# Sparse attention and two feed-forward layers on one core: a second buffer for the exponentials of a local unit, a free ScalarE order in the third tile, and high priority for the operations between h and y

## The chip, the cores and the metric

The program runs on one core of one Trainium2 chip. The metric is the device time of one execution in microseconds (us); lower is better. Several runs of a kernel agree within about 0.2%.

## The reference, cut to what matters

Four batches of 576 tokens pass through an attention with eight heads of 64 columns. Heads 0 to 3 see the last 32 positions, heads 4 to 7 every 32nd position. Two feed-forward layers follow.

```python
scores = scale * np.matmul(q, k.transpose(0, 1, 3, 2))
rel = pos[:, None] - pos[None, :]
mask_local = (rel >= 0) & (rel < 32)
mask_strided = (rel >= 0) & (pos[None, :] % 32 == pos[:, None] % 32)
attn = softmax(np.where(masks, scores, -1e9))      # local for heads 0..3, strided for 4..7
x = (attn @ v) as 2304 tokens x 512
h = np.maximum(x @ w_in, 0.0);  x = h * h @ w_out                    # 512 -> 2048 -> 512
h = x @ w_in2;  g = np.maximum(h, 0) + alpha * np.minimum(h, 0);  out = g @ w_out2
```

All inputs are 32-bit floats.

## The kernel before

**Tiles and steps.** The first layer works on seven tiles of tokens: the first three, t = 0, 1, 2, have 256 tokens, the next four 384. The second layer has six tiles of 384. The hidden width of 2048 is cut into 16 pieces f of 128. A step is one pair of tile and piece. Steps 0 to 31 alternate between tiles 0 and 1, steps 32 to 47 are the third tile (t = 2), steps 48 to 111 the tiles 3 to 6, and steps 112 to 207 the second layer.

**What one step does.** Every operand is split into a high part and a rest, and each product is three matmuls. `emit_h` makes h of a step with 12 matmuls (L566) in the one PSUM bank "h". `emit_g` makes g and its high part gh: in the first layer three ScalarE instructions, Relu (L578), Square into gh (L579), Square into g (L580). `emit_gl` makes the rest gl with one VectorE subtraction (L594). `emit_y` adds 8 matmuls with gh and 4 with gl into the banks y (L620). In the second layer `emit_g` has two Relus and a copy on ScalarE (L583, L584, L588) and one VectorE operation (L585). The tags g, gh and gl have two buffers each. The next h needs the bank that the Relu reads, so a Relu that comes late holds up the next h.

**Attention beside the steps.** The attention of a later tile is spread over the steps of an earlier one. A local unit goes through scores (PE, L245), `softmax_a` (VectorE: scaling and mask into e, L259, and the maximum, L263), `softmax_b` (ScalarE: one Exp for each block with its sum, L267), `softmax_c` (VectorE: L274, L275; then the division, from tile 3 on three ScalarE copies with a scale, L282, before that one VectorE product, L277), `turn` (PE transposes, L289, which read e), `turn_copy` (ScalarE, L293), `values` (PE, L299), `emit_hi` (ScalarE, L308) and `emit_lo` (VectorE, L315). The tag e has one buffer: the next unit's L259 waits until the transposes of the unit before have read e. The strided heads are done on VectorE alone in many products and sums (L450, L457, L491, L498), which fill its time. Units for tile 3 run in steps 32 to 47, with first stages in steps 32, 34, 37 and 40.

**Weights.** The first layer's weights arrive as 64-bit words and are converted in four parts, on ScalarE (L159, L162, L185) and VectorE (L171, L172, L175, L191), just ahead of their first use.

**What sets the order.** `run` emits the parts of step n in this order: loads, gl of n, `front`, h of n + 1, `fill`, the matmuls of attention, g of n + 1, `tail`, y of n. A scheduler then orders each engine's instructions before the program runs: among those that are ready in its own account of time it takes the one that was emitted first. `manual_schedule` names engines that keep the order of emission instead. Before the change that is SyncE alone in steps 0 to 31, and SyncE and ScalarE from step 32 on. Within `tc.high_priority()` instructions count as if they had been emitted at the start of the program. TensorE and VectorE are left to the scheduler throughout. Once set, the order of an engine is kept on the chip.

Of the kernel before, what the change touches and what calls it, by code (L numbers as in the profile page):

```python
# [16 lines left out]
P = 128  # L17
# [53 lines left out]
def attn_moe_moe2(  # L71
# [39 lines left out]
    NF = w_in1.shape[0]  # L111
# [31 lines left out]
    def load_w(layer, f):  # L143

        t = wpool.tile([P, 2, 512, 2], U32, tag=f"w{f}", name="wraw")
        for h in range(2):
            src = W[layer][h][f].bitcast(U32).rearrange("p (f t) -> p f t", t=2)
            nc.sync.dma_start(out=t[:, h], in_=src)
        raws[layer, f] = t
# [58 lines left out]
    class Unit:  # L208


        bufs = None
# [40 lines left out]

        def softmax_a(self):
            n = self.n
            self.e = self.new("e", [P, 3, 96], bufs=1)[:, 0:n]
            self.st = apool.tile([P, 3, 4], F32, tag="st", name="stat", bufs=4)[:, :, 0:n]
            s = self.s[:, 0:96 * n].rearrange("p (n c) -> p n c", c=96)
            m = mfirst if self.first else mloc
            nc.vector.scalar_tensor_tensor(  # L259
                out=self.e, in0=s, scalar=SCALE,  # L260
                in1=m.unsqueeze(1).to_broadcast([P, n, 96]), op0=ALU.mult, op1=ALU.add,
            )
            nc.vector.tensor_reduce(out=self.st[:, 0, :], in_=self.e, op=ALU.max, axis=AX.X, negate=True)  # L263
# [284 lines left out]
    steps = [(0, t, f) for t, f in FIRST]  # L548
# [6 lines left out]
    def cols_of(n):  # L555
        return COLS[steps[n][1]] if n < SECOND else T

    def emit_h(n):
        l, t, f = steps[n]
        xh, xl = x_tile(t) if l == 0 else x2[t]  # L560
        w = wslot[l, f]
        h = psum("h")
        for c in range(NC):
            whi, wlo = w[:, 0, c * P:(c + 1) * P], w[:, 1, c * P:(c + 1) * P]
            for i, (a, b) in enumerate(((whi, xh), (whi, xl), (wlo, xh))):
                nc.tensor.matmul(  # L566
                    h[:, 0:b.shape[2]], a, b[:, c, :], start=(c == 0 and i == 0), stop=(c == NC - 1 and i == 2)
                )
        hs[n] = h

    def emit_g(n):
        l, t, f = steps[n]
        m = cols_of(n)
        h = hs.pop(n)[:, 0:m]
        g = gpool.tile([P, T], F32, tag="g", name="g")[:, 0:m]
        gh = gpool.tile([P, T], F32R, tag="gh", name="gh")[:, 0:m]
        if l == 0:
            nc.scalar.activation(out=g, in_=h, func=AF.Relu)  # L578
            nc.scalar.activation(out=gh, in_=g, func=AF.Square)  # L579
            nc.scalar.activation(out=g, in_=g, func=AF.Square)  # L580
        else:
            u = spool.tile([P, T], F32, tag="pr", name="u", bufs=2)
            nc.scalar.activation(out=g, in_=h, func=AF.Relu)  # L583
            nc.scalar.activation(out=u, in_=h, func=AF.Relu, scale=-1.0)  # L584
            nc.vector.scalar_tensor_tensor(  # L585
                out=g, in0=u, scalar=nalpha[:, f:f + 1], in1=g, op0=ALU.mult, op1=ALU.add
            )
            nc.scalar.activation(out=gh, in_=g, func=AF.Copy)  # L588
        g_sb[n] = (g, gh)

    def emit_gl(n):
        g, gh = g_sb[n]
        gl = gpool.tile([P, T], F32R, tag="gl", name="gl")[:, 0:cols_of(n)]
        nc.vector.tensor_tensor(  # L594
            out=gl, in0=g, in1=gh.bitcast(F32), op=ALU.subtract
        )
        g_sb[n] = (gh, gl)
# [70 lines left out]
    def at(when, n, fn, *args):  # L668
        when.setdefault(n, []).append((fn, args))

    def emit(when, n):
        for fn, args in when.get(n, []):
            fn(*args)
# [79 lines left out]
    def run(ns):  # L753
        for n in ns:
            l, t, f = steps[n]
            emit(starts, n)
            emit(loads, n)
            emit_gl(n)
            emit(front, n)
            if n + 1 < len(steps):  # L760
                emit_h(n + 1)
            emit(fill, n)
            emit(tensor_part, n)
            if n + 1 < len(steps):
                emit_g(n + 1)
            emit(tail_part, n)
            emit_y(n)
            if f == NF - 1:
                evac(t, l)

    outs = {}
    with tc.manual_schedule(engines={mybir.EngineType.SP}):
        def part(tag, *sizes):

            whole = wpool.tile([P, sum(sizes)], F32, tag=tag, name=f"att_{tag}")
            return [whole[:, sum(sizes[:i]):sum(sizes[:i + 1])] for i in range(len(sizes))]

        masks, de11 = part("w11", 224, 512)
        mfirst, mstr = masks[:, 0:96], masks[:, 96:224]
        bufs = {}  # L780
        for t, tags in enumerate((("w7", "w8", "w9", "w10"), ("w15", "w14", "w13", "w12"))):
            n = D * (t + 1)
            a = part(tags[0], 640, 640, 384, 384)
            v = part(tags[1], *(512,) * 4)
            pt = part(tags[2], *(512,) * 4)
            d = part(tags[3], *((512, 512, 256, 256) if t == 0 else (768, 768, 512)))
            for p in range(2):
                bufs[t, "L", p] = {
                    "qk": a[p].rearrange("p (n c) -> p n c", c=D + 96), "v": v[p][0:96].rearrange("p (n c) -> p n c", c=P),
                    "e": a[2 + p].rearrange("p (n c) -> p n c", c=96), "pt": pt[p][0:96],  # L790
                }
                bufs[t, "D", p] = {
                    "qk": d[p], "v": v[2 + p][0:n].rearrange("p (n c) -> p n c", c=P),
                    "e": d[2 + p] if t == 0 or p == 0 else de11, "pt": pt[2 + p][0:n],
                }
        units = []
        for t, kind in ORDER:
            p = sum(isinstance(x, Unit if kind == "L" else Dense) and x.t == t for x in units)
            if kind == "L":
                units.append(Unit(t, p, 0))  # L800
                units[-1].bufs = bufs[t, "L", p]
            else:
                units.append(Dense(t, p, bufs[t, "D", p]))

        def load_consts():
            nc.sync.dma_start(out=ident, in_=consts[:, 0:128])
            nc.sync.dma_start(out=mloc, in_=consts[:, 128:224])
            nc.sync.dma_start(out=masks, in_=consts[:, 224:448])

        for i, x in enumerate(units):  # L810
            x.load_qk()
            if i == 0:
                load_consts()
            if i > 0:
                units[i - 1].load_v()
            for f, w in enumerate(LOAD_AFTER):
                if w == i:
                    load_w(0, f)
        units[-1].load_v()
        for f, w in enumerate(LOAD_AFTER):  # L820
            if w >= len(units):
                load_w(0, f)
        plan()

        todo = []
        for i, unit in enumerate(units):
            for j, (name, tick) in enumerate(STAGES):
                banks = BANKS.get(name)
                args = (banks[i % len(banks)],) if banks else ()
                todo.append((i + tick + (BACK if unit.t else 0), 1, i, j, getattr(unit, name), args))  # L830
        for f, ticks in enumerate(EARLY):
            for j, (fn, tick) in enumerate(zip((convert_a, convert_b, convert_c, convert_d), ticks)):
                todo.append((tick, 0, f, j, fn, (0, f)))
        for tick, *_, fn, args in sorted(todo, key=lambda x: x[:4]):
            n = sum(tick >= x for x in TICKS)
            if n:
                at(starts, n - 1, fn, *args)
            else:
                fn(*args)
        emit_h(0)  # L840
        emit_g(0)
        run(range(2 * NF))
    with tc.manual_schedule(engines={mybir.EngineType.SP, mybir.EngineType.Activation}):
        run(range(2 * NF, len(steps)))


_OUTS = [((2304, 512), "float32")]
# [104 lines left out]
```

## Time and profile before

| | |
|---|---|
| median of 3 runs | 895.06 us (894.0 to 895.51) |
| the profiled execution, its own time | 895.83 us |
| its span in the profile | 894.0 us, so 1.83 us lie around it |
| TensorE matmul busy | 870.4 us (97% of the span) |
| VectorE busy | 553.5 us (62%) |
| ScalarE busy | 455.1 us (51%) |
| mean granted TensorE clock | 0.996 |

The span runs from the first to the last instruction. PE is TensorE's matmul, PEld its weight load, DVE is VectorE, ACT ScalarE, POOL GpSimd, SP SyncE. The granted clock is a share of full speed: 1.00 is 2.4 GHz, and 0.5 would be 1.2 GHz throughout. Busy shares over the whole span mix a start that loads and converts weights, a first layer beside which attention runs, and a second layer that is matmul almost alone.

### The profile page before, as it was taken

The page shows a single profiled execution, that of the slowest core. Times are in us where ns is not written, and L with a number is a line of the kernel's source. Part 1 is how long each engine was busy: PE and PEld are TensorE (multiplying, and loading weights), DVE is VectorE, ACT ScalarE, POOL GpSimd, SP SyncE. Part 2 cuts the span into 40 slices and gives each one's busy share as a digit, 9 for nine tenths or more (in the row PEclk, how much of TensorE's full clock was granted, in tenths as well). Part 3 has the DMA queues.
Part 4 walks back from the last instruction along what each step waited for, and adds up shares of the span by engine and source line. Part 5 has one row for each costly group of instructions (what it writes and reads, how often), then busy time and mean ns, then how long its engine had stood idle before and what let it go on. Part 6 is the DMA issues. An engine that isn't in the chain of part 4 may idle for free.

```text
span 894.0 us, 13787 instructions
## 1 busy us (share of the span) xinstructions
PE 870.4 (97%) x5448; PEld 817.4 (91%) x5448; DVE 553.5 (62%) x877; ACT 455.1 (51%) x1063; POOL 1.5 (0%) x10
## 2 busy tenths in 40 slices
PE   6799999899999999999999999999999999999997
PEld 5699989799999999999999999999999999999996
DVE  5999999949678796794598983233233333333322
ACT  6889655455545554545577664334334334334332
POOL 0000000000000000000000000000000000000000
PEclk9999999999999999999999999999999999999999
DMA  9990402111212212100687200100100100100000
GB/s 295 393 339 2 153 8 86 45 52 62 71 51 73 68 56 73 49 8 26 241 271 267 82 10 27 36 9 29 34 10 30 33 10 30 33 9 32 5 1 36
DMA packets 33537, 70.34 MB, mean 79 GB/s; under 512 B 5696, under 2 KB 17600, under 8 KB 33472
## 3 DMA queue, kind: packets, MB, share of 16 engines
q1 hardware_dynamic: 33472, 69.46, 22.8%
q8 instruction: 43, 0.70, 0.3%
q14 instruction: 22, 0.18, 0.1%
HBM read 60.01 MB, written 9.44 MB: 78 GB/s over the span
## 4 chain that ended last, share of the span: by engine, by line
PE 88%; DMA 6%; DVE 4%; ACT 1%; issue 1%; SPq 0%; ACTq 0%; DVEq 0%
PE ps_y L620 42%; PE ps_h L566 42%; DMA wraw<-in_w1o_dram 2%; DMA att_w<-in_qd_dram 1%; PE ps_o L299 1%; PE ps_s L245 1%; DMA wraw<-in_w1i_dram 1%; DMA att_w<-in_v_dram 1%; PE ps_pt L289 1%; DVE pr L491 1%; DVE ss L457 1%; DVE w L191 0%; DVE so L498 0%; DVE pr L450 0%; DVE gl L594 0%
## 5 line engine op out<-in xcount | busy, mean ns | idle before, releaser
L566 PE MATMUL ps_h<-xh_c,w 128*128 128x384 f32 (+1 forms) x896 | 221.5, 316 | 4.6 <-ACT g L578 4.2
L566 PE MATMUL ps_h<-xh,w 128*128 128x384 f32 x768 | 212.5, 337 | 0.0
L585 DVE SCALAR_TENSOR_TENSOR g<-u,nalpha,g 128x384 f32<-128x384 f32 x96 | 59.3, 618 | 193.9 <-ACT u L584 193.9
L594 DVE TENSOR_TENSOR gl<-g,gh 128x384 fp32r<-128x384 f32 (+1 forms) x208 | 108.6, 523 | 107.8 <-ACT g L580 57.9
L566 PEld LDWEIGHTS ps_h<-xh_c,w 128*128 128x128 f32 x896 | 157.9, 191 | 7.1 <-ACT g L578 5.4
L620 PE MATMUL ps_y<-gh,w 128*128 128x384 f32 (+1 forms) x896 | 158.3, 319 | 0.0
L620 PE MATMUL ps_y<-w,gh 128*128 128x512 f32 x576 | 149.0, 394 | 0.1
L566 PEld LDWEIGHTS ps_h<-xh,w 128*128 128x128 f32 x768 | 140.4, 188 | 4.2
L566 PE MATMUL ps_h<-xl_c,w 128*128 128x384 f32 (+1 forms) x448 | 140.7, 314 | 0.0
L620 PEld LDWEIGHTS ps_y<-gh,w 128*128 128x128 f32 x896 | 138.7, 190 | 1.5
L583 ACT ACTIVATE g<-ps_h 128x384 f32<-128x384 f32 x96 | 47.2, 492 | 168.5 <-PE ps_h L566 168.2
L566 PE MATMUL ps_h<-xl,w 128*128 128x384 f32 x384 | 128.9, 336 | 0.0
L578 ACT ACTIVATE g<-ps_h 128x384 f32<-128x384 f32 (+1 forms) x112 | 49.4, 441 | 151.2 <-PE ps_h L566 146.6
L620 PEld LDWEIGHTS ps_y<-w,gh 128*128 128x128 f32 x576 | 106.6, 188 | 17.2 <-ACT gh L588 0.6
L620 PE MATMUL ps_y<-gl,w 128*128 128x384 f32 (+1 forms) x448 | 86.2, 313 | 2.0 <-DVE gl L594 1.9
L566 PEld LDWEIGHTS ps_h<-xl_c,w 128*128 128x128 f32 x448 | 85.5, 191 | 0.1
L588 ACT ACTIVATE gh<-g 128x384 fp32r<-128x384 f32 x96 | 50.5, 526 | 68.1 <-DVE g L585 68.1
L620 PE MATMUL ps_y<-w,gl 128*128 128x512 f32 x288 | 82.0, 392 | 0.0
L566 PEld LDWEIGHTS ps_h<-xl,w 128*128 128x128 f32 x384 | 72.1, 188 | 4.1
L620 PEld LDWEIGHTS ps_y<-gl,w 128*128 128x128 f32 x448 | 71.7, 189 | 2.6 <-DVE gl L594 2.6
L620 PEld LDWEIGHTS ps_y<-w,gl 128*128 128x128 f32 x288 | 54.1, 188 | 12.5
L579 ACT ACTIVATE gh<-g 128x384 fp32r<-128x384 f32 (+1 forms) x112 | 53.8, 480 | 2.9
(98 smaller groups left out, 840.7 us busy)
## 6 DMA issues: line engine op xcount, KB each, us to landing
wraw<-in_w1i_dram SPq DMA_DIRECT2D x16, 512.0 KB, 8.8
wraw<-in_w1o_dram SPq DMA_DIRECT2D x16, 512.0 KB, 9.1
wraw<-in_w2i_dram SPq DMA_DIRECT2D x16, 512.0 KB, 3.7
wraw<-in_w2o_dram SPq DMA_DIRECT2D x16, 512.0 KB, 4.7
qk<-in_qk_dram SPq DMA_DIRECT2D x16, 336.0 KB, 3.8
out_dram<-ev SPq DMA_DIRECT2D x18, 256.0 KB, 2.3
y<-ev SPq DMA_DIRECT2D x16, 192.0 KB, 2.0
x2raw<-y SPq DMA_DIRECT2D x16, 192.0 KB, 3.2
```

The lines of the kernel that those rows point to most:

```text
L245: nc.tensor.matmul(s, self.qk[:, j, 0:P], self.qk[:, j, P:], start=True, stop=True)
L289: nc.tensor.transpose(self.pt_ps[0:96, P * j:P * j + P], self.e[:, j, :], ident)
L299: nc.tensor.matmul(self.o[64 * h:64 * h + 64, 64 * j:64 * j + 64], self.v[:, j, D * h:D * h + D], self.pt[:, P * j + 64 * h:P * j + 64 * h ...
L457: nc.vector.tensor_reduce(out=self.s[:, b, r:r + ROWS, j0:j1], in_=pr, op=ALU.add, axis=AX.X)
L566: nc.tensor.matmul(h[:, 0:b.shape[2]], a, b[:, c, :], start=(c == 0 and i == 0), stop=(c == NC - 1 and i == 2))
L578: nc.scalar.activation(out=g, in_=h, func=AF.Relu)
L579: nc.scalar.activation(out=gh, in_=g, func=AF.Square)
L583: nc.scalar.activation(out=g, in_=h, func=AF.Relu)
L585: nc.vector.scalar_tensor_tensor(out=g, in0=u, scalar=nalpha[:, f:f + 1], in1=g, op0=ALU.mult, op1=ALU.add)
L588: nc.scalar.activation(out=gh, in_=g, func=AF.Copy)
L594: nc.vector.tensor_tensor(out=gl, in0=g, in1=gh.bitcast(F32), op=ALU.subtract)
L620: nc.tensor.matmul(y, a, b, start=(f == 0 and i == 0 and (l, t) != (0, 1)), stop=(f == NF - 1 and i == 2), skip_group_check=(l == 0 and t ...
```

## The change

The tag e gets two buffers. `emit_gl(n)` and `emit_g(n + 1)` are emitted with high priority in every step. The region in which only SyncE keeps the order of emission now reaches to step 47, so that ScalarE's order in the third tile is the scheduler's; from step 48 on it is as before. No instruction is added or taken away.

```diff
         def softmax_a(self):
             n = self.n
-            self.e = self.new("e", [P, 3, 96], bufs=1)[:, 0:n]
+            self.e = self.new("e", [P, 3, 96], bufs=2)[:, 0:n]
...
             emit(loads, n)
-            emit_gl(n)
+            with tc.high_priority():
+                emit_gl(n)
             emit(front, n)
...
             emit(tensor_part, n)
             if n + 1 < len(steps):
-                emit_g(n + 1)
+                with tc.high_priority():
+                    emit_g(n + 1)
             emit(tail_part, n)
...
         emit_h(0)
         emit_g(0)
-        run(range(2 * NF))
+        run(range(3 * NF))
     with tc.manual_schedule(engines={mybir.EngineType.SP, mybir.EngineType.Activation}):
-        run(range(2 * NF, len(steps)))
+        run(range(3 * NF, len(steps)))
```

## Rows read from the trace of the kernel before

**Rows 1.** Windows: stretch, its length, busy us (instructions) by engine, clock, DMA.

```profile
core 0: us, PE busy (x) PEld busy (x) DVE busy (x) ACT busy (x) POOL busy (x), PEclk, DMA share, GB/s
28.00:49.00 21.00, 17.02 (x188) 14.75 (x183) 19.31 (x38) 18.51 (x52) 0.00 (x0) 0.92 1.03 402
...
140.00:200.00 60.00, 55.80 (x469) 54.01 (x468) 45.48 (x79) 31.64 (x99) 0.28 (x1) 0.97 0.20 62
200.00:500.00 300.00, 300.00 (x1860) 294.71 (x1859) 238.58 (x342) 166.80 (x389) 0.28 (x1) 1.00 0.31 104
```

**Rows 2.** Waits of PE from 49 us on: total us, times, longest.

```profile
PE ps_h L566 <- ACT g L578: 4.2, 1, 4.2
PE ps_y L620 <- DVE gl L594: 1.9, 2, 1.7
```

**Rows 3.** Timeline of VectorE, 120 to 129 us: start, duration, instruction.

```profile
124.14 1.67 DVE L457 TENSOR_REDUCE ss<-pr 128x10 f32<-128x640 f32 x2
...
126.86 0.42 DVE L594 TENSOR_TENSOR gl<-g,gh 128x256 fp32r<-128x256 f32 x1
127.20 0.16 DVE L274 TENSOR_SCALAR stat<-stat 128x2 f32<-128x2 f32 x1
127.27 0.42 DVE L594 TENSOR_TENSOR gl<-g,gh 128x256 fp32r<-128x256 f32 x1
```

**Rows 4.** Timeline of ScalarE, 118 to 131 us.

```profile
120.64 0.42 ACT L580 ACTIVATE g<-g 128x256 f32<-128x256 f32 x1
```

**Rows 5.** Timeline of PE, 122 to 130 us; in brackets the idle time before.

```profile
127.33 0.74 PE L620 MATMUL ps_y<-gl,w 128*128 128x256 f32 x4 [1.66 <-DVE gl L594]
...
129.11 0.38 PE L289 MATMUL ps_pt<-ident,e 128*96 128x128 f32 x2
```

**Rows 6.** Timeline of ScalarE, 147 to 163 us.

```profile
147.71 0.42 ACT L580 ACTIVATE g<-g 128x256 f32<-128x256 f32 x1
148.03 0.36 ACT L267 ACTIVATE e<-e,stat 128x96 f32<-128x96 f32 x1
...
158.60 0.37 ACT L267 ACTIVATE e<-e,stat 128x96 f32<-128x96 f32 x1 [4.06 <-DVE stat L263]
...
161.48 0.90 ACT L282 ACTIVATE e<-e,stat 128x96 f32<-128x96 f32 x3 [1.70 <-DVE stat L275]
162.29 0.36 ACT L578 ACTIVATE g<-ps_h 128x256 f32<-128x256 f32 x1
```

**Rows 7.** Timeline of VectorE, 149 to 163 us.

```profile
156.97 0.45 DVE L259 SCALAR_TENSOR_TENSOR e<-ps_s,mloc 128x288 f32<-128x288 f32 x1
...
161.22 0.17 DVE L275 RECIPROCAL stat<-stat 128x3 f32<-128x3 f32 x1
```

**Rows 8.** Timeline of PE, 153 to 166 us.

```profile
155.82 0.28 PE L566 MATMUL ps_h<-xh_c,w 128*128 128x256 f32 x1
155.94 0.49 PE L289 MATMUL ps_pt<-ident,e 128*96 128x128 f32 x3
...
162.71 0.42 PE L566 MATMUL ps_h<-xh_c,w 128*128 128x256 f32 x1 [4.21 <-ACT g L578]
```

**Rows 9.** Windows right behind that wait, columns as in rows 1.

```profile
162.70:165.47 2.77, 2.76 (x14) 2.54 (x16) 2.77 (x4) 1.19 (x3) 0.00 (x0) 0.54 0.02 6
165.47:168.00 2.53, 2.53 (x27) 2.41 (x27) 2.53 (x4) 1.44 (x4) 0.00 (x0) 0.83 0.26 59
```

**Rows 10.** Timeline of PE, 28 to 49 us.

```profile
36.08 1.22 PE L620 MATMUL ps_y<-gh,w 128*128 128x256 f32 x8
...
41.43 0.69 PE L299 MATMUL ps_o<-att_w,att_w 96*64 96x64 f32 x16 [1.58 <-ACT att_w L293]
...
44.32 1.91 PE L620 MATMUL ps_y<-gh,w 128*128 128x256 f32 x8
```

**Rows 11.** Timeline of ScalarE, 208 to 214 us (first tile of 384).

```profile
212.83 0.91 ACT L282 ACTIVATE e<-e,stat 128x96 f32<-128x96 f32 x3 [1.48 <-DVE stat L275]
213.65 0.47 ACT L578 ACTIVATE g<-ps_h 128x384 f32<-128x384 f32 x1
```

**Rows 12.** The chain that ended last, 200 to 230 us: start, duration, instructions.

```profile
210.70 2.08 PE ps_h L566 x12
212.78 2.08 PE ps_y L620 x12
```

**Rows 13.** VectorE by line and shape, 200 to 484 us: count, busy us, mean ns.

```profile
L594 DVE TENSOR_TENSOR gl<-g,gh 128x384 fp32r<-128x384 f32 x63 | 34.8, 552 | 43.7 <-ACT g L580 43.7
L491 DVE TENSOR_TENSOR pr<-kv,ss 128x1024 f32<-128x1024 f32 x9 | 11.0, 1220 | 0.1
```

**Rows 14.** Timeline of ScalarE, 0 to 4 us.

```profile
0.73 1.28 ACT L267 ACT_TABLE_LOAD   x1 [0.73 <-PEq L933]
```

## The prediction

> **What bounds the kernel now.** I read the windows first, because the shares of the whole span mix stages. Between 200 and 500 us PE is busy for all 300 us at full clock [rows 1]; the chain that ended last is there nothing but h and y matmuls, 2.08 us for twelve of each [rows 12]. The reader is to see that nothing which makes VectorE or ScalarE quicker in this stretch can bring time: PE has no hole to close. The second layer is the same. So the change can gain only before 200 us, and what it gains there moves the whole rest forward. In the windows before 200 us the holes are in two places: 28 to 49 us, with PE busy 17.02 of 21 us and a clock of 0.92, and 140 to 200 us, with 55.80 of 60 us and 0.97 [rows 1].
>
> The second view is PE's waits from 49 us on. There are only two entries: one wait of 4.2 us of an h matmul for the Relu (L578), and two for gl (L594), together 1.9 us, of which the longest is 1.7 us [rows 2]. What the change can take away after 49 us is thus 6.1 us of waits and what the clock lost behind them. The timelines then say why each wait is there.
>
> **The wait of 1.66 us.** The Square into g of that step starts at 120.64 us and takes 0.42 [rows 4], so gl could run at 121.06. It runs at 126.86 [rows 3], 5.8 us late, behind strided sums and a weight conversion that were emitted earlier; VectorE is never idle here. The y matmuls that need it wait until 127.33 [rows 5]. The next gl follows at 127.27, also late.
>
> **The wait of 4.21 us.** The last h matmul of that step starts at 155.82 and takes 0.28, so the Relu could run at 156.10; it runs at 162.29 [rows 8, 6]. ScalarE stands idle for 4.06 us before an Exp, then for 1.70 us before the copies with a scale, and the Relu is queued behind both, because ScalarE keeps the order of emission [rows 6]. The Exp is late because L259 of that unit runs only at 156.97 [rows 7], after the transposes of the unit before, which start at 155.94 and read the only buffer e [rows 8]. The copies are late because L275 runs at 161.22 on a full VectorE [rows 7]. Then the clock: the two windows behind the wait show 0.54 over 2.77 us and 0.83 over 2.53 us [rows 9], so part of this stretch ran at 1.2 instead of 2.4 GHz.
>
> **The change part by part.** No instruction is added, so nothing has a price of its own except by its place.
>
> *High priority for gl and g.* In the first place gl moves from 126.86 to about 121.3, and the wait of 1.66 us has no cause left. What is late next: VectorE's other work moves back by what jumps ahead of it, here two subtractions of 0.42 us each [rows 3]. The transposes of a unit at 129.11 [rows 5] depend on that work through L274, which already stands behind the first of the two [rows 3]. PE would now reach them some 1.5 us earlier, while VectorE has the same sum of work before them. If PE's order keeps them where they are, all but 0.4 us of the 1.66 is given back; if the scheduler puts h ahead of them, nothing is. I take 1.0, with 0.4 and 1.66 as the bounds. The second, small wait for gl is worth the remaining 0.2 at most; I take 0.1.
>
> *ScalarE's order in the third tile and two buffers for e.* Either edit alone reaches the long wait. With ScalarE free and g first among what is ready, the Relu goes at 156.10 whatever the Exp waits for. With two buffers L259 need not wait for the transposes. I take all 4.2 us. The bound below: an order that the scheduler sets can again put a waiting instruction ahead of a Relu. The nearest row is the idle time of 1.70 us before the copies [rows 6]; 0 to 1.7 for that, and I take 0, since in steps 0 to 31, where ScalarE is already free, no PE wait for a Relu is among the entries after 49 us [rows 2].
>
> *The clock.* Without the hole PE should stay at full clock. What it lost is 2.77 x (1 - 0.54) = 1.27 and 2.53 x (1 - 0.83) = 0.43, together 1.7 us [rows 9]. The lower bound is 0, if another hole takes its place.
>
> *The start.* The order also changes between 28 and 49 us, where ScalarE is busy 18.51 and VectorE 19.31 of 21 us [rows 1]. Here g and gl jump ahead of attention and weight conversion. PE has holes, the longest 1.58 us before the values of a unit [rows 10], and behind them y matmuls run slowly: eight take 1.91 us against 1.22 before [rows 10]. Earlier g would fill such holes with y, worth up to the 1.58 and some 0.7 of clock, 2.3 together. But three ScalarE instructions of 0.36 to 0.42 us and one subtraction of 0.42 [rows 3, 6], 1.6 us in all, can stand in front of the unit whose values tile 1 waits for. Between a gain of 2.3 and a loss of 1.6 I take 0.
>
> *Elsewhere.* From step 48 on ScalarE keeps its order, so priority moves only VectorE's gl, by 0.55 us each, ahead of strided pieces of up to 1.22 [rows 13]. PE covers that: VectorE has 238.58 busy of 300 us [rows 1]. In the third tile it has 14.5 us of idle time in 60 [rows 1], so tile 3's attention should be ready although PE comes about 7 us earlier. If that cover were gone, each us that tile 3's x is late would be lost again.
>
> The sum: 1.0 + 0.1 + 4.2 + 1.7 = 7.0 us. The profiled execution took 895.83 (span 894.0 and 1.83 around it), so 888.8 on its scale. The median of the runs is 0.8 lower, 895.06, which gives 888.1.
>
> **The rivals.**
>
> *Only part of it.* The free order of ScalarE or PE leaves a new wait of about the size of the 1.70 us idle time, the first place gives back its 1.26, and the start loses part of 1.6. The result is 7.0 - 1.7 - 0.6 - 1.0 = 3.7 gained, about 891.4. For it speaks that VectorE is full around both places, and that PE's order is settled ahead by assumed durations. Against it: PE had only three waits in 845 us [rows 2].
>
> *The change doesn't do what it says.* If the scheduler in its own account sees gl ready only where it stands now, priority moves nothing in the first place, and if there the Exp of a unit still comes before the Relu, ScalarE's free order repeats the old one. Then the time stays within 1.5 us of 895.1. Two late subtractions within 0.41 us of each other [rows 3] would fit that account as well as a backlog. Against it: the second buffer removes the transposes from in front of L259 in any order.
>
> *Slower: the late Relu in the tiles from 48 on.* There ScalarE still waits in order. The copies of one unit wait 1.48 us for L275 and the Relu follows at 213.65 [rows 11], although its h ended at 212.78 [rows 12]: 0.87 late. It ends 0.47 later, at 214.12, and the y matmuls cover it until 214.86 [rows 12], so 0.74 us are left. Each gl that priority puts ahead of the unit's VectorE work costs 0.55 [rows 13]. One is hidden; two pass the cover by 0.36, three by 0.91. Three tiles of four units make twelve places. The mechanism decides from 7.0 / 12 = 0.58 us at each place on; with three it costs 10.9 us and gives 895.06 - 7.0 + 10.9, about 899.0. Against it: one gl is due in each step, and a unit's L274 and L275 fall within one step or two.
>
> *A table switch.* Leaving ScalarE's order free mixes Exp more freely with Square and Relu. The trace has one table load in the whole execution, 1.28 us at 0.73 us [rows 14], and an Exp directly behind a Square with no idle time between [rows 6], so the functions of this kernel share one set and no order adds a load. If they didn't, the four units of the third tile would need two loads each, 8 x 1.28 = 10.2 us on ScalarE, and with half of it seen by PE the time would be 895.06 - 7.0 + 5.1, about 893.2. The Trainium skill, "ScalarE: Activation LUTs", section "Table sets: the hidden batching unit", says to batch calls by table set and not by function, because each switch of sets costs a load; by that page's own price of about 2.66 us for a switch with its drain, eight would be 21 us, an estimate, and the change would be slower. The trace agrees that a load takes 1.28 us and shows that the rule's condition isn't met.
>
> **How the numbers follow.** A measurement of this kernel can tell about 0.2%, or 1.8 us, from no change. My forecast of 888.1, with its own range 885.5 to 890, has a chance of 0.60; its lower end is the forecast less the start's 2.3 and 0.3 for the first place. The partial gain (890 to 893.2) has 0.16, the table switch 0.01, an order that changes nothing 0.11, and slower 0.12: 0.06 for the late Relus, 0.06 for a start or a third tile that loses more than all the gains. Faster is 0.60 + 0.16 + 0.01 = 0.77, same 0.11, slower 0.12. The range reaches from 885.5 to 893.8, which takes in the partial gain and leaves out no change and slower.
>
> **What the profile after would show.** Right: no PE wait for L578 between 150 and 165 us, a granted clock of 1.00 there, gl within a us of its Square around 121 us, PE's waits after 49 us together under 1 us, and the first h of step 48 some 6 to 8 us earlier. Wrong: a PE wait for unit work (L289, L299 or L566 for the attention's x) around 129 or in the third tile; a later end of the stretch of holes, now at 49 us; or PE no longer full between 200 and 500 us, which would mean that gl's priority pushed unit work past its due time. The forecast would be most wrong if the start moved, since its term is the one that I could only bound.

## The result and the profile after

The changed kernel takes 888.9 us (median of 8 runs, 888.4 to 890.42), the kernel before 895.9 in the same comparison. The ratio is 0.9915, with a 95% interval from 0.9891 to 0.9938: faster by 0.6 to 1.1%. The forecast was 888.1, the range 885.5 to 893.8. Two of the eight runs of before, 901.84 and 903.8 us, lie well above the rest, by more than the 0.2% within which runs were said to agree; without them its median is 895.3 us and the gain 6.4 us instead of 7.0. The profiled execution took 890.42 us with a span of 888.6, so its span is 5.4 us shorter than before's.

First the windows of the kernel after (stretch, length, busy us and instructions by engine, clock, DMA), to hold against [rows 1].

```profile
core 0: us, PE busy (x) PEld busy (x) DVE busy (x) ACT busy (x) POOL busy (x), PEclk, DMA share, GB/s
28.00:49.00 21.00, 15.16 (x167) 13.30 (x168) 18.64 (x38) 17.67 (x49) 0.00 (x0) 0.93 1.03 402
...
140.00:200.00 60.00, 60.00 (x517) 59.20 (x516) 58.38 (x95) 34.23 (x109) 0.28 (x1) 1.00 0.29 87
200.00:500.00 300.00, 300.00 (x1850) 294.00 (x1849) 234.44 (x337) 165.46 (x385) 0.28 (x1) 1.00 0.29 101
```

From 140 to 200 us PE (TensorE's matmul) has no hole left, that is, no idle time, and the full clock. From 28 to 49 us it does less than before: 15.16 us busy in place of 17.02. So something was gained behind and something lost ahead. PE's waits say the same; first those of 28 to 49 us, then those from 49 us on (total us, times, longest), against [rows 2].

```profile
PE ps_o L299 <- ACT att_w L293: 2.1, 1, 2.1
PE ps_y L620 <- ACT gh L579: 1.4, 1, 1.4
...
PE ps_h L566 <- ACT g L578: 0.8, 1, 0.8
```

Both waits for gl and the wait of 4.21 us are gone. The one entry from 49 us on lies at 53.39 us, at the first h of step 4, and still belongs to the start. So the stretch of holes, which ended at 49 us before, ends 4.4 us later here (2.1 later in a second profile of this kernel); the prediction had named a later end as a sign of being wrong.

The timeline of VectorE in the kernel after (start, duration, instruction, idle time before), at three places:

```profile
29.12 0.69 DVE L172 SCALAR_TENSOR_TENSOR wt<-wraw 128x512 uint32<-128x512 uint32 x1
31.11 0.43 DVE L594 TENSOR_TENSOR gl<-g,gh 128x256 fp32r<-128x256 f32 x1 [1.31 <-ACT g L580]
31.46 0.69 DVE L175 SCALAR_TENSOR_TENSOR wt<-wraw,wt 128x512 uint32<-128x512 uint32 x1
...
124.63 0.42 DVE L594 TENSOR_TENSOR gl<-g,gh 128x256 fp32r<-128x256 f32 x1 [0.26 <-ACT g L580]
...
151.53 0.46 DVE L259 SCALAR_TENSOR_TENSOR e<-ps_s,mloc 128x288 f32<-128x288 f32 x1 [0.72 <-PE ps_s L245]
```

And ScalarE in the same kernel:

```profile
32.18 1.15 ACT L185 ACTIVATE w<-wt 128x512 fp32r<-128x512 f32 x2 [1.09 <-DVE wt L175]
...
124.18 0.42 ACT L580 ACTIVATE g<-g 128x256 f32<-128x256 f32 x1
...
154.71 0.37 ACT L267 ACTIVATE e<-e,stat 128x96 f32<-128x96 f32 x1
157.31 0.38 ACT L578 ACTIVATE g<-ps_h 128x256 f32<-128x256 f32 x1 [1.17 <-PE ps_h L566]
159.98 0.91 ACT L282 ACTIVATE e<-e,stat 128x96 f32<-128x96 f32 x3 [1.10 <-DVE stat L275]
160.79 0.36 ACT L578 ACTIVATE g<-ps_h 128x256 f32<-128x256 f32 x1
```

At 124 us gl follows its Square at once; before it came 5.8 us late [rows 3, 4]. At 151.53 L259 waits for its own scores and no longer for the transposes, its unit's Exp runs at 154.71, and the Relu at 157.31 waits only for its h matmuls; before, these three stood at 156.97, 158.60 and 162.29 [rows 6, 7]. At 31.11 the price is to be seen: the first gl stands in front of L175 while its Square has not run, VectorE idles 1.31 us, and L185, which needs L175, comes after an idle time of 1.09 us on ScalarE. In the kernel before, VectorE ran L175 first and had no idle time there:

```profile
27.15 0.69 DVE L172 SCALAR_TENSOR_TENSOR wt<-wraw 128x512 uint32<-128x512 uint32 x1
27.76 0.68 DVE L352 TENSOR_REDUCE stat<-att_w 128x4 f32<-128x512 f32 x1
28.36 0.68 DVE L175 SCALAR_TENSOR_TENSOR wt<-wraw,wt 128x512 uint32<-128x512 uint32 x1
28.96 0.55 DVE L259 SCALAR_TENSOR_TENSOR att_w<-ps_s,mloc 128x384 f32<-128x384 f32 x1
29.42 0.41 DVE L594 TENSOR_TENSOR gl<-g,gh 128x256 fp32r<-128x256 f32 x1
```

### The profile page after: what moved, and what is told of

Read it like the earlier page. It is cut to its first block, busy times and chain, and to the rows that moved or that the text cites. A ratio compares the mean times of both kernels' runs of the same rounds, so it can differ in the third digit from the quotient of the medians.

```text
span 888.6 us, 13786 instructions
## 1 busy us (share of the span) xinstructions
PE 868.0 (98%) x5448; PEld 816.5 (92%) x5448; DVE 553.9 (62%) x877; ACT 453.6 (51%) x1063; POOL 1.5 (0%) x10
## 4 chain that ended last, share of the span: by engine, by line
PE 95%; ACT 2%; DMA 1%; SPq 0%; issue 0%; DVE 0%; ACTq 0%
PE ps_h L566 45%; PE ps_y L620 45%; PE ps_s L245 1%; PE ps_o L299 1%; DMA att_w<-in_qd_dram 1%; PE ps_pt L289 1%; ACT wraw L159 0%; ACT w L185 0%; ACT att_w L267 0%; PE ps_y L385 0%; PE ps_pt L372 0%; ACT att_w L356 0%; PE ps_s L340 0%; PE ps_y L340 0%; PE ps_o L385 0%
## 5 line engine op out<-in xcount | busy, mean ns | idle before, releaser
L566 PE MATMUL ps_h<-xh_c,w 128*128 128x384 f32 (+1 forms) x896 | 220.2, 314 | 2.0 <-ACT g L578 0.8
L566 PE MATMUL ps_h<-xh,w 128*128 128x384 f32 x768 | 212.4, 337 | 0.0
L566 PEld LDWEIGHTS ps_h<-xh_c,w 128*128 128x128 f32 x896 | 156.9, 189 | 3.6 <-ACT w L185 1.6
L566 PEld LDWEIGHTS ps_h<-xh,w 128*128 128x128 f32 x768 | 140.4, 188 | 4.2
L566 PE MATMUL ps_h<-xl_c,w 128*128 128x384 f32 (+1 forms) x448 | 139.9, 312 | 0.0
L566 PE MATMUL ps_h<-xl,w 128*128 128x384 f32 x384 | 129.0, 336 | 0.0
L566 PEld LDWEIGHTS ps_h<-xl_c,w 128*128 128x128 f32 x448 | 84.8, 189 | 0.1
L566 PEld LDWEIGHTS ps_h<-xl,w 128*128 128x128 f32 x384 | 72.1, 188 | 4.1
L580 ACT ACTIVATE g<-g 128x384 f32<-128x384 f32 (+1 forms) x112 | 53.8, 481 | 2.8
```

What stands on the lines that cost most here:

```text
L566: nc.tensor.matmul(h[:, 0:b.shape[2]], a, b[:, c, :], start=(c == 0 and i == 0), stop=(c == NC - 1 and i == 2))
```

## The experiments

To compare stages I measure from the first h matmul (L566) of one step to that of another. The stage lengths below are differences of such start times, worked out from each trace and good to about 0.02 us; the last stage ends at the first h of step 207. The clock is that of steps 0 to 4. All are in us; median and ratio are of the timed runs, each against the kernel before in the same comparison (895.9 to 896.6). So two comparisons can be 0.7 us apart by that alone, and most of the intervals overlap: where two kernels differ by 1 to 2 us, the argument rests on the stages, and the medians only go with it.

```
                     0-4 (clock)    4-24   24-48   48-207  median  ratio [95%]
before               27.19 (0.94)  62.15   86.85   684.16
after                29.58 (0.94)  61.31   78.00   684.13  888.90  0.9915 [0.9891, 0.9938]
after again          29.68 (0.94)  61.49   78.00   684.13  888.79  0.9907 [0.9874, 0.9940]
priority_alone       29.58 (1.00)  61.31   80.70   684.12  891.69  0.9953 [0.9926, 0.9980]
no_priority          25.92 (1.00)  62.28   81.73   684.93  890.64  0.9934 [0.9907, 0.9961]
free_alone           25.93 (1.00)  62.17   81.05   684.42  891.27  0.9946 [0.9916, 0.9976]
two_buffers_alone        -         62.16   81.22   683.74  889.94  0.9929 [0.9899, 0.9959]
late_priority        27.03 (0.94)  61.18   80.38   684.13  888.65  0.9905 [0.9873, 0.9938]
priority_gl_only     27.85 (1.00)  61.94   78.44   684.13  888.43  0.9895 [0.9842, 0.9948]
first_gl_in_turn         -         61.29   77.98   684.13  887.10  0.9885 [0.9836, 0.9934]
late_less_vector     27.04 (0.94)  61.14   78.38   685.18  887.63  0.9894 [0.9855, 0.9933]
less_vector_alone    29.60 (1.00)  61.50   78.05   685.07  890.81  0.9935 [0.9908, 0.9962]
late_two_steps       27.04 (0.94)  61.14   77.89   684.23  885.21  0.9864 [0.9828, 0.9899]
late_gl_less_vector  27.04 (0.94)  62.72   78.81   684.81  889.09  0.9903 [0.9867, 0.9938]
```

In the traces of two_buffers_alone and of first_gl_in_turn step 4 begins at 55.6 and 57.8 us, in the others between 47.6 and 53.4; their first stage is left out of the table, and they are read from step 4 on.

### The changed kernel once more (after again)

No edit; it shows how much of a stage is scatter.

> The changed kernel once more. If the 2.4 us that the stretch from the first h of step 0 to the first h of step 4 grew by (27.19 us before, 29.58 in the profile after) belong to the change, this run shows 29 to 30 us there again; the rival, that they are scatter between executions, expects about 27 to 28. The first h of step 0, 2.0 us later in the profile after, is scatter by both and may lie anywhere between 21.8 and 23.9 us. Time by both: 0.8 to 0.9% below the kernel before.

Measured: 888.79 us. The stages agree within 0.2 us with those of the first profile. Only the first h of step 0 lies elsewhere, at 21.46 us against 23.81 (expected between 21.8 and 23.9). So the gain of 24 to 48 and the loss of 0 to 4 both come back, and what lies ahead of step 0 scatters. The rival, that the longer start is scatter, is ruled out.

### High priority alone (priority_alone)

```diff
+            with tc.high_priority():
+                emit_gl(n)
...
+                with tc.high_priority():
+                    emit_g(n + 1)
```

> High priority alone; one buffer for e, and ScalarE in order from step 32 on. Theory: the wait for gl near 125 us goes (1.7), the start loses 2.4, and the wait for the Relu near 158 us stays with its clock (4.2 and 1.7), since the Exp and the scaled copies still stand ahead of the Relu on ScalarE: within 1.5 us of the kernel before, no clear difference. Rival (priority of gl and g is enough to bring the Relu forward): about 6 us below the kernel before.

Measured: 891.69 us, 4.5 below before, between what the theory and what the rival expected. I had expected the long wait to stay; it did not. PE and ScalarE in the third tile of this kernel:

```profile
151.60 0.58 PE L289 MATMUL ps_pt<-ident,e 128*96 128x128 f32 x3
...
159.67 0.39 PE L566 MATMUL ps_h<-xh_c,w 128*128 128x256 f32 x1 [0.88 <-ACT g L578]
```

```profile
158.44 0.91 ACT L282 ACTIVATE e<-e,stat 128x96 f32<-128x96 f32 x3 [2.19 <-DVE stat L275]
159.26 0.36 ACT L578 ACTIVATE g<-ps_h 128x256 f32<-128x256 f32 x1
```

The transposes of the first unit run at 151.60, ahead of the h matmuls of step 36; before they stood behind those of step 37 and started at 155.94 [rows 8]. So the one buffer e was free in time, and of the wait of 4.21 us 0.88 is left, caused by the Relu that is still queued behind L282. High priority on ScalarE and VectorE thus also moved work on PE that it does not name. The gain of 24 to 48 (6.15 us) is bought with a start of 29.58 us.

### A second buffer and a free ScalarE, without priority (no_priority)

```diff
-            self.e = self.new("e", [P, 3, 96], bufs=1)[:, 0:n]
+            self.e = self.new("e", [P, 3, 96], bufs=2)[:, 0:n]
...
-        run(range(2 * NF))
+        run(range(3 * NF))
```

> Two buffers for e and ScalarE free in the third tile, without high priority. Theory: the wait for the Relu and its clock go (5.9 us), the wait for gl of 1.7 us stays, the start is that of before: about 5.9 us, 0.66%, below the kernel before. Rival (without priority a free ScalarE puts the Exp or the copies ahead of the Relu again): a gain of 2 us or less, with a PE wait for L578 in the third tile.

Measured: 890.64 us. PE's waits from 49 us on in this kernel:

```profile
PE ps_y L620 <- DVE gl L594: 1.9, 2, 1.7
PE ps_h L566 <- ACT g L578: 0.7, 2, 0.4
```

The waits for gl are there unchanged, the wait of 4.21 us is not; two short ones for a Relu remain. So the long wait needs no priority, and the wait for gl yields to neither of the other two edits.

### The free ScalarE alone (free_alone)

```diff
-        run(range(2 * NF))
+        run(range(3 * NF))
```

> ScalarE free in the third tile alone; one buffer for e, no high priority. Theory (either edit alone reaches the long wait): like the run with both, steps 32 to 40 in about 29 us instead of 33.5, 4.5 to 6 us below the kernel before. Rival (the Exp of the one buffer still comes late, and the scheduler puts it ahead of a Relu): a PE wait for L578 of over 2 us in the third tile, a gain of 3 us or less.

Measured: 891.27 us. The Relu that was late (step 37) now waits only for its own h matmuls. ScalarE, then PE's waits from 49 us on:

```profile
156.59 0.39 ACT L578 ACTIVATE g<-ps_h 128x256 f32<-128x256 f32 x1 [1.59 <-PE ps_h L566]
```

```profile
PE ps_y L620 <- DVE gl L594: 1.9, 2, 1.7
PE ps_h L566 <- ACT g L578: 0.2, 1, 0.2
```

### Two buffers alone (two_buffers_alone)

```diff
-            self.e = self.new("e", [P, 3, 96], bufs=1)[:, 0:n]
+            self.e = self.new("e", [P, 3, 96], bufs=2)[:, 0:n]
```

> Two buffers for e alone; ScalarE in order from step 32 on, no high priority. Theory: L259 of the second unit runs at about 151 instead of 157 us, the Exp follows at once, and only the scaled copies can still wait for L275: the wait for the Relu falls from 4.2 us to 0 to 1.7, a gain of 4 to 6 us. Rival (the scaled copies are what holds the Relu, and VectorE is full): the wait stays above 2 us, a gain of 3 us or less.

Measured: 889.94 us, 6.6 below before, a little more than expected. PE's only waits from 56 us on are the two for gl, together 1.9 us; none for a Relu. Each of the two edits alone removes the long wait, and 24 to 48 takes 81.05, 81.22 and, with both, 81.73 us: the second of them adds nothing.

### Priority from step 4 on (late_priority)

```diff
-            with tc.high_priority():
+            with (tc.high_priority() if n >= 4 else ExitStack()):
                 emit_gl(n)
...
-                with tc.high_priority():
+                with (tc.high_priority() if n >= 4 else ExitStack()):
                     emit_g(n + 1)
```

> The changed kernel with high priority only from step 4 on, so that the start keeps the order of before. Theory (priority costs the start 2.4 us): from the first h of step 0 to that of step 4 about 27.2 us, the rest as after, and a time about 2.4 us below the changed kernel, 1.1% below the kernel before. Rival (the start is scatter): the time of the changed kernel within 1 us.

Measured: 888.65 us, no better than the changed kernel and 2 us above what I had expected. The start is back at 27.03 us, 2.6 less. But 24 to 48 takes 80.38 in place of 78.00. PE, then VectorE of this kernel around 128 us:

```profile
128.77 0.50 PE L566 MATMUL ps_h<-xh_c,w 128*128 128x256 f32 x2 [0.80 <-DVE w L191]
...
130.70 0.38 PE L566 MATMUL ps_h<-xh_c,w 128*128 128x256 f32 x1 [0.47 <-ACT g L578]
```

```profile
125.57 0.43 DVE L594 TENSOR_TENSOR gl<-g,gh 128x256 fp32r<-128x256 f32 x1
125.91 1.67 DVE L457 TENSOR_REDUCE ss<-pr 128x10 f32<-128x640 f32 x2
127.50 1.22 DVE L191 TENSOR_TENSOR w<-wt,w 128x1024 fp32r<-128x1024 f32 x1
```

PE reached this place earlier, VectorE was still busy with strided sums without a gap, and the last weight conversion (L191) came late for h. So what the start gave was lost again, by this trace to a full VectorE; the kernels with less work on VectorE below test that.

### Priority for gl alone (priority_gl_only)

```diff
             if n + 1 < len(steps):
-                with tc.high_priority():
-                    emit_g(n + 1)
+                emit_g(n + 1)
```

> The changed kernel with high priority for gl alone, not for g. Theory (the wait near 125 us is VectorE's, so gl is what matters; the start is lost by g on ScalarE): no PE wait for L594, steps 0 to 4 in 27 to 28 us instead of 29.6, a time within 1.5 us of the changed kernel. Rival (gl's priority reorders the start by itself): steps 0 to 4 stay at 29 to 30 us.

Measured: 888.43 us, the same as the changed kernel. Its start is at full clock and takes 27.85 us. That is 1.9 more than the 25.92 of no_priority at the same clock. With g's priority as well it is 29.58 (priority_alone), another 1.7 more. VectorE of this kernel has the same gap as the changed one:

```profile
29.51 0.42 DVE L594 TENSOR_TENSOR gl<-g,gh 128x256 fp32r<-128x256 f32 x1 [1.30 <-ACT g L580]
29.85 0.68 DVE L175 SCALAR_TENSOR_TENSOR wt<-wraw,wt 128x512 uint32<-128x512 uint32 x1
```

Without g's priority 4 to 24 and 24 to 48 are longer by 0.6 and 0.4 us. So g's priority gives about 1.0 later on and takes 1.7 in the start. How it takes them, ScalarE shows, first in priority_alone, then in priority_gl_only:

```profile
34.70 0.39 ACT L578 ACTIVATE g<-ps_h 128x256 f32<-128x256 f32 x1
34.96 0.39 ACT L267 ACTIVATE att_w<-att_w,stat 128x96 f32<-128x96 f32 x1
...
39.08 0.61 ACT L375 ACTIVATE att_w<-ps_pt 128x512 f32<-128x512 f32 x1
```

```profile
35.73 0.36 ACT L578 ACTIVATE g<-ps_h 128x256 f32<-128x256 f32 x1
36.09 0.60 ACT L375 ACTIVATE att_w<-ps_pt 128x512 f32<-128x512 f32 x1
```

With g's priority the Relu stands ahead of the four Exps of a unit (L267) and the two Squares among them; without it the Relu follows the Exps. The copy L375, which other attention matmuls (L385) wait for, comes 16.5 us after the first h of step 0 instead of 13.9. That is the kind of loss which the prediction had named for the start. The path from there to the 1.7 us was not followed further.

### The first gl in its turn (first_gl_in_turn)

```diff
-            with tc.high_priority():
+            with (tc.high_priority() if n >= 1 else ExitStack()):
                 emit_gl(n)
```

> The changed kernel, with the gl of step 0 alone taken out of high priority; all other gl and every g keep it. Theory: the start is longer because that one gl stands on VectorE ahead of L175 while its Square has not run, so that VectorE idles 1.31 us and the weight L185 behind it comes 1.1 us late. Then L175 runs without that idle time, steps 0 to 4 take 27.2 to 28.3 us in place of 29.6, and the total is 1.3 to 2.4 us under the changed kernel's 888.8, if the later stages stay as they are. Rival: the start is lost to the sum of all jumps, g's above all; then steps 0 to 4 stay above 29 us and the total within 0.6 us of 888.8.

Measured: 887.10 us, 1.7 below the changed kernel, within what the theory expected and outside the rival's 0.6. From step 4 on the trace is the changed kernel's (within 0.05 us in each stage), so the gain can only lie ahead of step 4. There VectorE runs L175 directly behind L352, with no idle time:

```profile
34.49 0.68 DVE L352 TENSOR_REDUCE stat<-att_w 128x4 f32<-128x512 f32 x1
35.09 0.68 DVE L175 SCALAR_TENSOR_TENSOR wt<-wraw,wt 128x512 uint32<-128x512 uint32 x1
```

The expected length of steps 0 to 4 can't be tested by this trace, in which everything from step 0 on is late: they take 32.18 us. The nearest like it is two_buffers_alone, with the first h of step 0 at the same place (25.59 us against 25.65), the same clock of 1.00 and no priority: 29.95 us. The difference of 2.2 us, against 3.7 between priority_alone and no_priority, makes the gain 1.4 us, an estimate. So one instruction of 0.43 us, put first, cost about 1.7 us by the medians and 1.4 by the two traces.

### Less work on VectorE ahead of step 32

`STRIDED_AT` says for a tile by how many steps from its base step its strided parts begin and end. For tile 3 the base is step 32, so -8 begins at step 24. Begun later, the parts should leave VectorE time for the last weights. Four kernels, with the edits as differences from the kernel that is named.

First with priority from step 4 on, and the parts of tile 3 four steps later (late_less_vector):

```diff
-STRIDED_AT = {2: (4, 24), 3: (-8, 13)}
+STRIDED_AT = {2: (4, 24), 3: (-4, 13)}
```

> High priority from step 4 on, and tile 3's strided work begun four steps later (step 28 instead of 24), so that VectorE has less to do while tile 1 ends. Theory (the 2.3 us that the start gains with late priority are given back between steps 24 and 32 because VectorE is full there): steps 24 to 32 fall from 27.5 to about 25.3 us, no PE wait for L191 near 129 us, and the time is about 2 us below the changed kernel, some 886.5 us. Rival (the give-back has another cause): steps 24 to 32 stay above 27 us and the time is that of the changed kernel. A third outcome, a new wait before step 48 because tile 3's attention comes too late, would show as a PE wait in steps 40 to 48.

Measured: 887.63 us, 1.1 above what I had expected. 24 to 48 is back at 78.38 us with the short start kept, and there is no wait for L191, as the theory has it; 1.05 us are lost again in 48 to 207. About 0.7 of that lies in steps 48 to 56 (36.77 us against 36.09 in the changed kernel). There ScalarE keeps the order of emission, and the Relu of step 51 stands behind copies that wait for L275. ScalarE in this kernel:

```profile
205.26 0.90 ACT L282 ACTIVATE e<-e,stat 128x96 f32<-128x96 f32 x3 [3.25 <-DVE stat L275]
206.07 0.47 ACT L578 ACTIVATE g<-ps_h 128x384 f32<-128x384 f32 x1
```

It runs 2.6 us after its h has ended; in before it was 0.9 [rows 11, 12], in the changed kernel 1.5. That is the late Relu which the prediction had as its slower rival, at one place: steps 51 and 52 take 9.66 us against 9.35. Why the rest is lost, and why L275 comes later there, was not followed. The third outcome, a wait in steps 40 to 48, came as well, with 0.3 us.

Then the same line in the changed kernel, with its priority from step 0 on (less_vector_alone):

```diff
-STRIDED_AT = {2: (4, 24), 3: (-8, 13)}
+STRIDED_AT = {2: (4, 24), 3: (-4, 13)}
```

> The changed kernel, with tile 3's strided work begun four steps later and nothing else. Control for the run with late priority and less vector work. Theory (a full VectorE between steps 24 and 32 matters only to a PE that comes there early): steps 0 to 4 in 29.6 us, steps 24 to 32 in 25.2 as in the changed kernel, and its time within 1 us. Rival (the later strided work is a gain by itself): 1 us or more below the changed kernel.

Measured: 890.81 us, 2.0 above the changed kernel and so worse than expected. 24 to 48 is the same (78.05 against 78.00); 0.9 us lies in 48 to 207, 0.7 of it in steps 48 to 56 as in the run above; 0.4 can be the comparison, in which before was slower by that much too (896.63 against 896.24); the rest of the difference I can't place. The control still holds: less strided work helps only where PE comes early.

Then priority from step 4 on again, and the parts only two steps later (late_two_steps):

```diff
-STRIDED_AT = {2: (4, 24), 3: (-8, 13)}
+STRIDED_AT = {2: (4, 24), 3: (-6, 13)}
```

> High priority from step 4 on, tile 3's strided work begun two steps later instead of four. Theory: VectorE has half of the relief, so steps 24 to 32 lie between 25.0 and 27.5 us, and steps 40 to 48 nearer to 26.4 than to 27.0; a time of 887 to 888.5 us. Rival (the relief works by which instruction stands first and not by how much work there is): steps 24 to 32 at one of the two ends.

Measured: 885.21 us (884.2 to 886.53), the best of all: 1.4% under the kernel before and 3.6 us under the changed kernel, all of whose runs lie at 888.16 us or above, though the two intervals of the ratio overlap. By the stages it is 2.7 to 3.0 us. I had expected 887 to 888.5, with half of the relief in steps 24 to 32; they take 25.04 us, as long as with four steps (25.04) and at one end of the range. That is the sign that the rival had named: it speaks for the order of the instructions there, and against the amount of work. The loss behind step 48 is gone as well (684.23 us). Its trace lists no wait of PE from 49 us on, and its windows are full from 100 us:

```profile
100.00:140.00 40.00, 40.00 (x347) 39.33 (x346) 38.81 (x68) 24.92 (x68) 0.28 (x1) 1.00 0.21 67
140.00:200.00 60.00, 60.00 (x507) 59.07 (x506) 57.43 (x93) 32.82 (x104) 0.28 (x1) 1.00 0.29 83
```

Last, late_less_vector with g taken out of high priority (late_gl_less_vector):

```diff
             if n + 1 < len(steps):
-                with (tc.high_priority() if n >= 4 else ExitStack()):
-                    emit_g(n + 1)
+                emit_g(n + 1)
```

> High priority for gl alone and from step 4 on, two buffers, ScalarE free in the third tile, tile 3's strided work begun four steps later. Theory (gl is the part that matters): steps 0 to 4 in about 27 us, no PE wait for L594 of over 0.3 us after 49 us, and the time of the same kernel with priority for g as well, 887.6, within 1 us. Rival (g's priority carries part of the gain): 1 us or more above it, with PE waits for L578 or L579.

Measured: 889.09 us, 1.5 above the same kernel with g's priority. 4 to 24 takes 62.72 us against 61.14, and two of its three PE waits for a Relu, 1.1 us together, lie there: gl is in time by its own priority, but the Relu is late again. That is what the rival expected. So g's priority carries a part of the gain, and from step 4 on the start does not pay for it.

## Why the prediction held, step by step

The total came out 0.8 us from the forecast, and that it came so near is in part luck: it is a sum of errors that partly cancel. By the two profiles: steps 4 to 24 got 0.84 us shorter and 24 to 48 got 8.85 shorter, 9.7 together where the prediction had 7.0; steps 0 to 4 got 2.39 longer where it had 0. That leaves 7.3 us gained against 7.0. (The first h of step 0 came 2.0 us later in the profiled execution of after than in that of before, which is why the spans differ by 5.4 only; in the second profile of after it came 0.35 earlier than in before. So the first h of step 48 came 5.3 us earlier in the one and 7.4 in the other, where the prediction had 6 to 8.)

**The wait of 1.66 us: right, under-sized.** I took 1.0 of it, and the range's lower end allowed 0.3 more, though the bound of 1.66 would have been 0.66 more. All of it went: steps 24 to 32 have PE busy 24.68 of 26.34 us before and 25.23 of 25.23 after. This hole lies in neither of the two stretches in which the prediction said that the holes are, but in a third window of before, which the prediction passed over:

```profile
100.00:140.00 40.00, 38.34 (x327) 37.34 (x327) 39.27 (x65) 22.10 (x60) 0.28 (x1) 1.00 0.19 65
```

The bound of 0.4, PE reaching the transposes too early, did not come true in the changed kernel. late_priority showed the like at a neighbouring place: PE earlier by the 2.6 us of the start, and VectorE not ready, there with a weight (L191) instead of a unit's work.

**The wait of 4.21 us: right.** It went in full, and with each of the two edits alone too, but for 0.2 us of waits for a Relu with the free ScalarE alone, as the prediction said of both. What it did not see is that priority alone takes most of it, through PE's order.

**The clock: right.** The same matmuls of steps 24 to 48 (684 recorded in each trace) kept PE busy for 80.99 us before and 78.00 after: 2.99 us, where I took 1.7. The clock of 0.95 over the 33.51 us from step 32 to 40 accounts for 1.7 of it, the whole term. The other 1.3 is no matter of the clock, and the prediction had no term for it. About 0.6 of it lies in steps 40 to 48, where 240 matmuls take 27.00 us before and 26.39 after, both at full clock and with no idle time listed. It is a wait that hides in busy time. PE, then ScalarE before:

```profile
175.25 0.84 PE L289 MATMUL ps_pt<-ident,e 128*96 128x128 f32 x3
```

```profile
174.82 0.91 ACT L282 ACTIVATE e<-e,stat 128x96 f32<-128x96 f32 x3 [1.75 <-DVE stat L275]
```

Three transposes take 0.84 us here and 0.49 at 155.94 us [rows 8]: here they start at 175.25, 175.52 and 175.78 us, each 0.05 us after the end of its own scaled copy. From the first of them to the next matmul 0.80 us pass, against 0.25 at 155.94: that is 0.55 of the 0.6. The remaining 0.7 was not traced.

**Elsewhere: right from step 48 on.** 48 to 207 took 684.13 us against 684.16, so the late Relus of the slower rival cost nothing. At one place, step 51, the Relu is indeed later than before (1.5 us after its h instead of 0.9), and that was covered. Steps 4 to 24 gained 0.84, for which there was no term but the 0.1 of the small wait for gl; half of it is small holes of PE (0.42 us before, none after), among them that wait.

**The start: the term that was wrong.** The prediction weighed a gain of 2.3 against a loss of 1.6 and took 0. The loss was 2.4 us at a clock of 0.94 and 3.7 at full clock (29.58 against 25.92), beyond its bound both times. It had priced what jumps ahead by the durations of the instructions, 0.36 to 0.42 us each. It missed that a jumped instruction need not be ready: in the order fixed ahead, gl stood in front of L175, and VectorE, full at this stage, idled 1.31 us for it, with L185 and the weights behind it. The priority of every gl accounts for 1.9 us at equal clock, and the first gl alone for about 1.7 of the total by first_gl_in_turn (1.4 by the traces). The priority of g accounts for the other 1.7, and there the prediction was right in kind: ScalarE's three instructions stand in front of a unit's work, priced at 1.2 of its 1.6 us.

**The rivals.** Only part of it, the kernel unchanged in effect, and a slower kernel by late Relus are ruled out by the stages above. The table switch is, too: the trace after has one table load, 1.28 us at 0.73 us, as before [rows 14]. The Trainium skill, "ScalarE: Activation LUTs", section "Table sets: the hidden batching unit", prices only switches between sets, and the trace agrees that a freer order within one set adds none.

## What to carry to other kernels

High priority is no free reordering: where an engine's order is fixed ahead, it can put an instruction that is not ready in front of the others on a full engine. Here the cost was that engine's idle time (1.31 us) and what was queued behind it, about 1.7 us in all, and not the instruction's own 0.43 us. So look in the profile after, in every stage that gets the priority, for idle time on a full engine in front of a jumped instruction, and take that one out. Time won early is kept only if the next full engine keeps up; here the 2.6 us of the start came through when VectorE's strided work was begun two steps later, not at all without that, and in part when it was begun four steps later. And a stage that is busy throughout may still hold waits: compare how long the same instructions take at two places.

## What the runs showed of the hardware that was not expected

The clock of the same early stretch differs from execution to execution. In the order without early priority, steps 0 to 4 took 27.03 to 27.19 us at 0.94 and 25.92 at 1.00. With early priority they took 29.58 to 29.68 at 0.94 and 29.58 to 29.60 at 1.00: at the higher clock TensorE only waits longer (holes of 6.75 us in the changed kernel at 0.94, 8.04 in priority_alone at 1.00). Among these waits are those of h for weights that VectorE and ScalarE convert, 1.3 us for L191 and 0.5 for L185 in priority_alone; that they set the length of the stretch fits this, but no run shows it by itself.
